# Depthwise-separable 1x1: preparing the weights in PSUM or in SBUF, one pw load ahead of x, smaller first chunks

## The chip, the cores and the metric

The kernel runs on one core of a Trainium2 chip. The metric is the device time of one execution in microseconds (us); less is better. TensorE (PE) multiplies, VectorE (DVE), ScalarE (ACT) and GpSimd (POOL) work on elements, SyncE (SP) issues most of the transfers. A time or a view of the trace counts from the start of the profiled span.

## What is computed

With a depthwise kernel of 1x1 the reference is a scaling of the channels followed by a matrix product over them:

```python
# x: (1, 384, 384, 384) bf16, dw: (1, 1, 384) bf16, pw: (384, 384) bf16
out = x * dw[0, 0][None, None, None, :]
return jnp.einsum('bhwc,cd->bhwd', out, pw)
```

The kernel scales the weights instead of x: out = x @ (diag(dw) pw), 147,456 rows of 384 channels. x is 113 MB, and so is the output.

## The kernel before

The rows are done in steps of 512, called supertiles here, 288 of them. Of each, DVE transposes 32x32 blocks of channel pairs (a bf16 pair moves as one 32-bit word), so that channels come to lie on partitions; PE multiplies, four row groups of 32 partitions side by side; ACT copies the result from PSUM; SP loads x and stores the output in chunks of several supertiles.

The four row groups each need all weights on their own 32 partitions, and even and odd channels apart. So the kernel makes `w_r`, 128 partitions of 6 blocks x 2 parities x 384 columns, in which each quadrant of 32 partitions holds the same weights, already times dw. It makes all six blocks with PE: a selection matrix, scaled by dw, times the rows of pw, into PSUM, and from there to SBUF by ACT and DVE.

The chunks of the first supertiles, and the loads that come first:

```python
head, tail = [[1, 1, 2, 2, 4]], [[6, 4], [4, 1, 1, 1, 1]]   # supertiles per load; groups of 10 between
...
nc.scalar.dma_start(dw_row[:], dw...).then_inc(s_dw, 16)
nc.sync.dma_start(pw_n[:, 0], pw[0:P, :]).then_inc(s_pw, 16)
nc.sync.dma_start(pw_n[:, 1:3], pw[P:C, :].rearrange("(k p) d -> p k d", p=P)).then_inc(s_pw2, 16)
load_x(0)
...                                          # then the other x loads and the stores, in order
```

The order of the weights in a supertile on PE; 12 steps of four matmuls each:

```python
w_first = {(0, 0): [(0, 1), (1, 3)], (4, 0): [(1, 4)], (4, 1): [(1, 5)]}   # weights that must be there
steps = [(b, par) for b in range(4) for par in range(2)] + [(4, 0), (5, 0), (4, 1), (5, 1)]

def supertile(s, rv):
    for b, par in steps:
        for q in range(4):
            if q == 0 and par == 0 and b in (0, 3):
                nc.tensor.wait_ge(s_t[s][b // 3], rv)          # half of the transposed x
            if q == 0 and s == 0:
                for e, v in w_first.get((b, par), []):
                    nc.tensor.wait_ge(s_wr[e], v)
            mm = nc.tensor.matmul(PS[s][:, q, :D],
                lhsT=Ts[s][32*q : 32*q+32, b, par::2], rhs=w_r[32*q : 32*q+32, b, par, :], ...)
```

What PE does ahead of the first supertile. `idle_work` multiplies constants by constants, so that PE is busy:

```python
idle_work(4)
nc.tensor.wait_ge(s_dw, 16)
for k in range(3):                       # dw from a row to a column: three 1x1 products into PSUM
    ...
mm.then_inc(s_df)
idle_work(2)
nc.tensor.wait_ge(s_pw, 16)
times = {(2, 0): 2, (2, 1): 2}           # these are done twice over, with the same result
for k in range(3):
    if k == 1:
        nc.tensor.wait_ge(s_pw2, 16)
    nc.tensor.wait_ge(s_sw, k + 1)
    for r in range(2):
        if k == 2:
            nc.tensor.wait_ge(*w_done[r])
        for v in [0, 1] * times.get((k, r), 1):
            mm = nc.tensor.matmul(PS[(k + 1) % 2][:, 2 * r + v, :D],
                lhsT=sel_w[64*v : 64*v+64, k, r, :, :]..., rhs=pw_n[64*v : 64*v+64, k, :], ...)
        mm.then_inc(s_w)
```

DVE builds the selection matrices, and ACT (five times) and DVE (once) take two banks of PSUM at a time to `w_r`; then DVE transposes the first two supertiles:

```python
w_eng = [1, 0, 1, 1, 1, 1]               # 1: ACT, 0: DVE
...
nc.vector.wait_ge(s_df, 1)
nc.vector.tensor_copy(dw_f[:], PS[1][:, 0, D : D + 3]).then_inc(s_dwf)
nc.vector.wait_ge(s_dwf, 2)
for k in range(3):
    nc.vector.tensor_scalar_mul(sel_w[:, k], sel[:]..., dw_f[:, k : k + 1]).then_inc(s_sw)
for i in range(6):
    w_out(i)                             # w_r[:, 2k : 2k+2, r, :] <- PSUM, 128x768
transposes(*order[0])
transposes(*order[1])
```

In the main loop DVE transposes supertile j + 2 as soon as PE is through with the buffer of supertile j.

Of the kernel before, what the change touches and what calls it, by code (L numbers as in the profile page):

```python
# [8 lines left out]
F32 = mybir.dt.float32  # L9
# [3 lines left out]
LMAX = 10  # L13
# [4 lines left out]
def _groups(n_super: int):  # L18

    head, tail = [[1, 1, 2, 2, 4]], [[6, 4], [4, 1, 1, 1, 1]]  # L20
    mid = n_super - sum(map(sum, head + tail))
    assert mid > 0 and mid % LMAX == 0
    return head + [[LMAX]] * (mid // LMAX) + tail
# [3 lines left out]
def kernel(  # L27
# [12 lines left out]
    nc = tc.nc  # L40
    P = nc.NUM_PARTITIONS
    B, H, W, C = x.shape
    assert dw.shape[0] == 1 and dw.shape[1] == 1, "only k=1 depthwise supported"
    D = pw.shape[1]
# [10 lines left out]
    chunks, first = [], 0  # L55
# [19 lines left out]
    sel_w = raw[:, 3 * D :].rearrange("p (k r q w) -> p k r q w", r=2, q=4, w=32)  # L75
    w_k = raw[:, 0 : 2 * D].rearrange("p (r d) -> p r d", d=D)
    eye = consts.tile([P, P], BF16, name="eye")
    sel = consts.tile([P, 2, 32], F32, name="sel")
    w_r = consts.tile([P, NB, 2, D], BF16, name="w_r")
    dw_row = consts.tile([1, C], BF16, name="dw_row")  # L80
    dw_f = consts.tile([P, 3], F32, name="dw_f")
    warm = consts.tile([P, 2], F32, name="warm")
# [6 lines left out]
    Ts = [bufp.tile([P, NB, 256], BF16, name=f"T{i}") for i in range(2)]  # L89
    Os = [bufp.tile([P, 4 * LMAX * D], BF16, name=f"O{i}") for i in range(NR)]  # L90
    PS = [psum.tile([P, 4, 512], F32, name=f"ps{s}") for s in range(2)]

# [8 lines left out]
    s_o = [nc.alloc_semaphore(f"s_o{i}") for i in range(NR)]  # L101
    s_dw = nc.alloc_semaphore("s_dw")
    s_pw = nc.alloc_semaphore("s_pw")
    s_pw2 = nc.alloc_semaphore("s_pw2")
    s_df = nc.alloc_semaphore("s_df")
# [3 lines left out]
    s_w = nc.alloc_semaphore("s_w")  # L109
    s_wr = [nc.alloc_semaphore(f"s_wr{e}") for e in range(2)]  # L110

    with tc.tile_critical(sync_engine=mybir.EngineType.Pool, no_gpsimd_drain=True):  # L112
# [60 lines left out]

        w_eng = [1, 0, 1, 1, 1, 1]
        w_all = [(s_wr[e], w_eng.count(e)) for e in range(2)]

        nc.scalar.dma_start(dw_row[:], dw.rearrange("a e c -> a (e c)")).then_inc(s_dw, 16)
        nc.sync.dma_start(pw_n[:, 0], pw[0:P, :]).then_inc(s_pw, 16)  # L178
        nc.sync.dma_start(pw_n[:, 1:3], pw[P:C, :].rearrange("(k p) d -> p k d", p=P)).then_inc(s_pw2, 16)  # L179
        load_x(0)  # L180

        todo = []
# [5 lines left out]
        for _, f, a in sorted(todo, key=lambda a: a[0]):  # L188
            if f is load_x and chunks[a[0]][4] == LMAX and chunks[a[0]][0] == 1:
                nc.sync.wait_ge(x_of(1)[1], 16)  # L190
            if f is store and a == (0, 0):

                for _ in range(28):
                    nc.sync.wait_ge(s_pw, 16)
            f(*a)
# [7 lines left out]

        w_done = [(s_wr[e], w_eng[: i + 1].count(e)) for i, e in enumerate(w_eng)]

        w_first = {(0, 0): [(0, 1), (1, 3)], (4, 0): [(1, 4)], (4, 1): [(1, 5)]}

        def w_ps(i):
            return PS[0 if i in (2, 3) else 1][:, 2 * (i % 2) : 2 * (i % 2) + 2, :D]


        steps = [(b, par) for b in range(4) for par in range(2)] + [(4, 0), (5, 0), (4, 1), (5, 1)]

        def supertile(s, rv):
            for b, par in steps:
                for q in range(4):
                    if q == 0 and par == 0 and b in (0, 3):
                        nc.tensor.wait_ge(s_t[s][b // 3], rv)
                    if q == 0 and s == 0:
                        for e, v in w_first.get((b, par), []):  # L220
                            nc.tensor.wait_ge(s_wr[e], v)
                    mm = nc.tensor.matmul(  # L222
                        PS[s][:, q, :D],
# [23 lines left out]

        idle_work(4)

        nc.tensor.wait_ge(s_dw, 16)  # L250
        for k in range(3):
            mm = nc.tensor.matmul(
                PS[1][:, 0, D + k : D + k + 1],
                lhsT=dw_row[:, P * k : P * k + P],
                rhs=ones[0:1, 0:1],
                start=True,
                stop=True,
            )
        mm.then_inc(s_df)
        idle_work(2)  # L260
        nc.tensor.wait_ge(s_pw, 16)
        times = {(2, 0): 2, (2, 1): 2}
        for k in range(3):
            if k == 1:
                nc.tensor.wait_ge(s_pw2, 16)
            nc.tensor.wait_ge(s_sw, k + 1)
            for r in range(2):
                if k == 2:
                    nc.tensor.wait_ge(*w_done[r])

                for v in [0, 1] * times.get((k, r), 1):
                    mm = nc.tensor.matmul(  # L272
                        PS[(k + 1) % 2][:, 2 * r + v, :D],
                        lhsT=sel_w[64 * v : 64 * v + 64, k, r, :, :].rearrange("p q w -> p (q w)"),
                        rhs=pw_n[64 * v : 64 * v + 64, k, :],
                        start=True,
                        stop=True,
                        tile_position=(64 * v, 0),
                    )
                mm.then_inc(s_w)  # L280
        with nc.tensor.Fori(0, NS // 2 - 1, 1) as it:
# [21 lines left out]
        for m in range(4):  # L303
# [11 lines left out]


        nc.gpsimd.affine_select(  # L317
            out=eye[:],
# [5 lines left out]
            channel_multiplier=1,  # L324
        ).then_inc(s_sel)
        for sem, v in w_all:
            nc.gpsimd.wait_ge(sem, v)
# [9 lines left out]
        for s in range(2):  # L337
            nc.scalar.copy(warm[:, s : s + 1], nc.const_aps.tensor(0.0, [P, 1], F32)).then_inc(s_a[s])  # L338

        def transposes(t, j):  # L340
# [17 lines left out]
            for h in range(2):  # L358
                if h == 0 and j == 0:
                    nc.vector.wait_ge(sem, n)  # L360
                ins = nc.vector.transpose(  # L361
                    out=Tw[:, 3 * h : 3 * h + 3],
                    in_=Xw[:, :, j, 96 * h : 96 * h + 96].rearrange("p k (b w) -> p b k w", w=32),
                )
                if jj >= 2:
                    ins._wait_ge(s_pe, 2 * (jj - 2) + h + 1)
                ins.then_inc(s_t[s][h])
# [5 lines left out]

        def w_out(i):
            e, k, r = w_eng[i], i // 2, i % 2
            out, in_ = w_r[:, 2 * k : 2 * k + 2, r, :], w_ps(i)
            o = nc.vector.tensor_copy(out, in_) if e == 0 else nc.scalar.copy(out, in_)  # L377
            o._wait_ge(s_w, i + 1)
            o.then_inc(s_wr[e])

# [5 lines left out]
            axis=mybir.AxisListType.X,  # L386
        ).then_inc(s_dwf)
        nc.vector.wait_ge(s_df, 1)
        nc.vector.tensor_copy(dw_f[:], PS[1][:, 0, D : D + 3]).then_inc(s_dwf)
        nc.vector.wait_ge(s_dwf, 2)  # L390
        for k in range(3):
            nc.vector.tensor_scalar_mul(
                sel_w[:, k], sel[:].unsqueeze(2).to_broadcast([P, 2, 4, 32]), dw_f[:, k : k + 1]
            ).then_inc(s_sw)
        for i in range(6):
            w_out(i)
        transposes(*order[0])
        transposes(*order[1])

# [62 lines left out]
```

## Time and profile before

| | |
|---|---|
| time, median of three runs | 573.68 us (573.62 to 574.42) |
| span of the profiled run | 571.9 us |
| PE busy | 567.0 us (99%) |
| DVE busy | 505.4 us (88%) |
| ACT busy | 418.4 us (73%) |
| DMA, mean over the span | 397 GB/s |
| first main matmul (kernel line 222) | 6.52 us |

The shares of the page are averages over the span, and nearly all of it is the main loop. The change concerns the first microseconds, so the views by time count here: the chain of work that ended last, and the timeline of each engine. L222 is the main matmul, L361 the transpose, L377 the copy of the weights from PSUM, L272 the matmul that makes them, L178 and L179 the loads of pw, L389 the copy of dw from PSUM, L392 the scaling of the selection matrices. A name with q (SPq) is the engine's sequencer, which issues the loads.

### The profile page before, as it was taken

To read this page: it belongs to the slowest core of one execution; us is meant where nothing else is said; L and a number is where in the kernel's file an instruction comes from. 1 tells how busy PE (TensorE), PEld (TensorE's weight loads), DVE (VectorE), ACT (ScalarE), POOL (GpSimd) and SP (SyncE) were. 2 spreads that over 40 slices of the span, in tenths; PEclk is the share of its full clock that TensorE was granted. 3 is DMA by queue.
4 is the path that set the end of the run, shared out by engine and by line. 5 is a ranking of instruction groups with operands and counts; after the bars stand their busy time and mean duration, and the time that the engine had idled before them with its cause. 6 is when DMAs were issued, how large, how long until landed. Compare 5 with 4: busy or idle time off the path is not lost.

```text
span 571.9 us, 29705 instructions
## 1 busy us (share of the span) xinstructions
PE 567.0 (99%) x13843; PEld 380.0 (66%) x13843; DVE 505.4 (88%) x586; ACT 418.4 (73%) x298; POOL 13.9 (2%) x41
## 2 busy tenths in 40 slices
PE   9999999999999999999999999999999999999997
PEld 4666666666666666666666666666666666666664
DVE  6889889889889889889889889889889889889885
ACT  6777777777777777777777777777777777777775
POOL 2042000000000000000000000000000000000000
PEclk9999999999999999999999999999999999999999
DMA  8999999999999999999999999999999999998677
GB/s 328 445 393 414 426 416 428 437 426 411 430 416 420 388 396 432 388 390 396 433 382 396 418 415 408 397 416 414 395 403 428 387 394 402 420 393 351 285 287 263
DMA packets 26740, 226.88 MB, mean 397 GB/s; under 512 B 1385, under 2 KB 7274, under 8 KB 22890
## 3 DMA queue, kind: packets, MB, share of 16 engines
q1 hardware_dynamic: 25796, 225.91, 97.4%
q10 hardware_dynamic: 934, 0.89, 0.4%
q14 instruction: 9, 0.07, 0.0%
q8 instruction: 1, 0.02, 0.0%
HBM read 113.54 MB, written 113.25 MB: 397 GB/s over the span
## 4 chain that ended last, share of the span: by engine, by line
PE 98%; DMA 1%; SPq 0%; DVE 0%; issue 0%; ACT 0%; POOLq 0%
PE ps L222 98%; DMA X<-in_x_dram 1%; PE ps L307 0%; PE ps L295 0%; DVE T L361 0%; ACT O L416 0%; SPq L179 0%; SPq L178 0%; SPq L457 0%; POOLq L112 0%; POOLq L446 0%
## 5 line engine op out<-in xcount | busy, mean ns | idle before, releaser
L222 PE MATMUL ps<-w_r,T 32*128 32x384 bf16 x13776 | 559.8, 321 | 0.2 <-DVE T L361 0.2
L361 DVE STREAM_TRANSPOSE T<-X 128x384 uint32<-128x384 uint32 x572 | 498.1, 874 | 58.2 <-DMA X<-in_x_dram 2.1
L421 ACT CAST O<-ps 128x1536 bf16<-128x1536 f32 x286 | 411.4, 1438 | 147.0 <-PE ps L222 147.0
L222 PEld LDWEIGHTS ps<-w_r,T 32*128 32x128 bf16 x13776 | 377.2, 93 | 183.1 <-issue 0.9
L336 POOL COPY Xk<-Xl 32x256 bf16<-32x256 bf16 x16 | 6.3, 394 | 0.0
L335 POOL COPY Xk<-Xl 32x128 bf16<-32x128 bf16 x16 | 4.6, 287 | 25.2 <-DMA Xl<-in_x_dram 24.3
L377 ACT CAST w_r<-ps 128x768 bf16<-128x768 f32 x5 | 3.6, 820 | 0.8 <-PE ps L272 0.8
L330 POOL COPY raw<-w_r 32x768 bf16<-32x768 bf16 x4 | 3.3, 819 | 6.4 <-ACT w_r L377 6.2
L239 PE MATMUL ps<-const-bfloat16-1.0 32*128 32x384 bf16 x24 | 2.2, 516 | 1.1 <-PEq L446 1.1
L272 PE MATMUL ps<-raw 64*128 64x384 bf16 x16 | 2.9, 513 | 0.1
L338 ACT ACT_TABLE_LOAD x1 | 1.3, 1283 | 1.5 <-PEq L446 1.5
L272 PEld LDWEIGHTS ps<-raw 64*128 64x128 bf16 x16 | 0.8, 113 | 2.2 <-DMA raw<-in_pw_dram 1.2
L412 DVE CAST O<-ps 128x384 bf16<-128x384 f32 x2 | 1.0, 552 | 1.4 <-PE ps L222 1.4
L361 DVE STREAM_TRANSPOSE T<-Xl 128x384 uint32<-128x384 uint32 x2 | 1.8, 876 | 0.2
L239 PEld LDWEIGHTS ps<-const-bfloat16-1.0 32*128 32x128 bf16 x24 | 0.7, 117 | 1.4 <-issue 1.4
L349 DVE STREAM_TRANSPOSE T<-Xk 128x384 uint32<-128x384 uint32 x2 | 1.2, 578 | 0.5 <-PE ps L222 0.4
L382 DVE TENSOR_REDUCE sel<-eye 128x64 f32<-128x128 bf16 x1 | 0.3, 290 | 1.5 <-POOL eye L317 1.5
L307 PE MATMUL ps<-raw,T 128*128 128x384 bf16 x8 | 1.5, 327 | 0.0
L416 ACT CAST O<-ps 128x384 bf16<-128x384 f32 x2 | 1.0, 478 | 0.7 <-PE ps L307 0.7
L377 DVE CAST w_r<-ps 128x768 bf16<-128x768 f32 x1 | 1.0, 958 | 0.5 <-PE ps L272 0.5
L416 DVE CAST O<-ps 128x384 bf16<-128x384 f32 x2 | 1.1, 558 | 0.1
L411 ACT CAST O<-ps 128x384 bf16<-128x384 f32 x2 | 0.9, 482 | 0.5 <-PE ps L222 0.5
(13 smaller groups left out, 4.5 us busy)
## 6 DMA issues: line engine op xcount, KB each, us to landing
X<-in_x_dram SPq DMA_DIRECT2D x26, 3840.0 KB, 21.9
out_dram<-O SPq DMA_DIRECT2D x26, 3840.0 KB, 27.9
X<-in_x_dram SPq DMA_DIRECT2D x3, 1536.0 KB, 18.5
out_dram<-O SPq DMA_DIRECT2D x4, 768.0 KB, 7.7
out_dram<-O SPq DMA_DIRECT2D x2, 1536.0 KB, 13.7
X<-in_x_dram SPq DMA_DIRECT2D x1, 2304.0 KB, 20.2
out_dram<-O SPq DMA_DIRECT2D x1, 2304.0 KB, 11.1
X<-in_x_dram SPq DMA_DIRECT2D x4, 384.0 KB, 4.4
```

The source lines that it names most:

```text
L222: mm = nc.tensor.matmul(PS[s][:, q, :D], lhsT=Ts[s][32 * q : 32 * q + 32, b, par::2], rhs=w_r[32 * q : 32 * q + 32, b, par, :], start=(b, ...
L239: nc.tensor.matmul(PS[0][:, 2 * (i % 2) + i // 2, :D], lhsT=ones[32 * i : 32 * i + 32, 0:P], rhs=ones[32 * i : 32 * i + 32, :], start=True ...
L272: mm = nc.tensor.matmul(PS[(k + 1) % 2][:, 2 * r + v, :D], lhsT=sel_w[64 * v : 64 * v + 64, k, r, :, :].rearrange("p q w -> p (q w)"), rhs ...
L307: mm = nc.tensor.matmul(PS[1][:, m, :D], lhsT=Tk[:, P * (m + 2) : P * (m + 3), par], rhs=w_k[:, par, :], start=False, stop=par == 1,)
L330: nc.gpsimd.tensor_copy(w_k[quads[n]], w_r[quads[n], n]).then_inc(s_wk)
L335: nc.gpsimd.tensor_copy(Xk[quads[n], g:8:4, :], x_b).then_inc(s_xk)
L336: nc.gpsimd.tensor_copy(Xk[quads[n], 8 + g : 24 : 4, :], Xl[quads[g], :, 64 * n : 64 * n + 64]).then_inc(s_xk)
L338: nc.scalar.copy(warm[:, s : s + 1], nc.const_aps.tensor(0.0, [P, 1], F32)).then_inc(s_a[s])
L361: ins = nc.vector.transpose(out=Tw[:, 3 * h : 3 * h + 3], in_=Xw[:, :, j, 96 * h : 96 * h + 96].rearrange("p k (b w) -> p b k w", w=32),)
L377: o = nc.vector.tensor_copy(out, in_) if e == 0 else nc.scalar.copy(out, in_)
L416: o = (nc.scalar.copy if n % 2 else nc.vector.tensor_copy)(Ov[:, n, j, :], PS[s][:, n, :D])
L421: a = nc.scalar.copy(Ov[:, :, j, :], PS[s][:, :, :D])
```

## The change

Six things are changed, all ahead of or in the first supertiles:

1. The last third of pw (channels 256 to 383) no longer goes through PE and PSUM. It is loaded four times, once to each quadrant of 32 partitions (two loads from SP, two from ACT, into a part of an output buffer that isn't in use yet), and scaled in SBUF by DVE (even channels) and POOL (odd channels). The scales for it come from four tiny matmuls and a copy by ACT.
2. The other weights leave PSUM one bank at a time (128x384), six by ACT and two by DVE, and PE's first supertile waits for each block where it needs it; its order of blocks is changed to suit.
3. The first 256 rows of pw are one load, and x0 is issued right after it.
4. The scaling of the selection matrices reads dw from PSUM; the copy of dw is gone.
5. The first half of the first transpose is done in three pieces with a signal each.
6. The chunks of x at the start are smaller: 1, 1, 1, 1, 2, 4 and then 5, 5, in place of 1, 1, 2, 2, 4 and 10.

It is meant to let PE begin, and go through, the first supertile earlier. The diff, cut to its core:

```diff
-    head, tail = [[1, 1, 2, 2, 4]], [[6, 4], [4, 1, 1, 1, 1]]
+    head, tail = [[1, 1, 1, 1, 2, 4], [5, 5]], [[6, 4], [4, 1, 1, 1, 1]]
 ...
+    w_d = Os[2][:, 0 : 4 * D].rearrange("p (b e) -> p b e", b=2)
 ...
-        nc.sync.dma_start(pw_n[:, 0], pw[0:P, :]).then_inc(s_pw, 16)
-        nc.sync.dma_start(pw_n[:, 1:3], pw[P:C, :].rearrange("(k p) d -> p k d", p=P)).then_inc(s_pw2, 16)
+        nc.sync.dma_start(pw_n[:, 0:2], pw[0 : 2 * P, :].rearrange("(k p) d -> p k d", p=P)).then_inc(s_pw, 16)
         load_x(0)
+        def load_w(eng, q):
+            rows = pw[2 * P : C, :].rearrange("(b i r) d -> i b (r d)", b=2, r=2)
+            eng.dma_start(w_d[32 * q : 32 * q + 32], rows).then_inc(s_wd, 16)
+        for q in range(2, 4):
+            load_w(nc.sync, q)
 ...
+        w_first = {
+            (0, 0): [(0, 2), (1, 2)], (2, 0): [(1, 3)], (3, 0): [(1, 4)], (2, 1): [(1, 5)], (3, 1): [(1, 6)],
+            (4, 0): [(0, 3)], (4, 1): [(2, 1)], (5, 0): [(0, 4)], (5, 1): [(2, 2)],
+        }
+        steps = [(b, par) for b in range(2) for par in range(2)]
+        steps += [(2, 0), (3, 0), (2, 1), (3, 1)] + [(b, par) for b in (4, 5) for par in range(2)]
 ...                                                     # in supertile(), for the first one
+                        if par == 0 and b in (1, 2):
+                            nc.tensor.wait_ge(s_tb, b)
 ...                                                     # PE ahead of the first supertile
-        idle_work(4)
+        idle_work(3)
 ...
-        idle_work(2)
+        idle_work(4)
         nc.tensor.wait_ge(s_pw, 16)
-        times = {(2, 0): 2, (2, 1): 2}
+        times = {(1, 1): 4}
+        nc.tensor.wait_ge(s_sw, 1)
+        copies(0, 0)                                     # copies(k, r): the matmuls as before, into PS[k]
+        nc.tensor.wait_ge(s_sw, 3)
+        for r in range(2):
+            for v in range(2):                           # scales of the last third: four products of one column
+                mm = nc.tensor.matmul(PS[1][:, 2 + v, D + 4 + r : D + 5 + r], lhsT=sel_w[..., 2, r, ...], rhs=ones[...])
+        mm.then_inc(s_df)
+        copies(0, 1)
+        copies(1, 0)
+        nc.tensor.wait_ge(s_dk, 1)
+        copies(1, 1)
 ...                                                     # POOL
+        nc.gpsimd.wait_ge(s_dk, 1)
+        nc.gpsimd.wait_ge(s_wd, 64)
+        for b in range(2):
+            w_scale(nc.gpsimd, b, 1).then_inc(s_wr[2])
 ...                                                     # ACT, after its table load and two small copies
+        for q in range(2):
+            load_w(nc.scalar, q)
 ...                                                     # DVE, first supertile
+                if h == 0 and jj == 0:
+                    for b in range(3):
+                        x_b = Xw[:, :, 0, 32 * b : 32 * b + 32]
+                        nc.vector.transpose(out=Tw[:, b], in_=x_b).then_inc(s_tb if b else s_t[0][0])
+                    continue
 ...
-        nc.vector.tensor_copy(dw_f[:], PS[1][:, 0, D : D + 3]).then_inc(s_dwf)
         for k in range(3):
-                sel_w[:, k], sel[:]..., dw_f[:, k : k + 1]
+                sel_w[:, k], sel[:]..., PS[1][:, 3, D + k : D + k + 1]
-        for i in range(6):
-            w_out(i)
+        nc.scalar.wait_ge(s_df, 2)
+        nc.scalar.copy(dw_k..., PS[1][:, 2:4, D + 4 : D + 6]).then_inc(s_dk)
+        for b, r in ((0, 0), (0, 1), (2, 0), (3, 0), (2, 1), (3, 1)):
+            w_out(1, b, r)                               # ACT: w_r[:, b, r, :] <- one bank, 128x384
+        for r in range(2):
+            w_out(0, 1, r)                               # DVE
         transposes(*order[0])
+        nc.vector.wait_ge(s_dk, 1)
+        nc.vector.wait_ge(s_wd, 64)
+        for b in range(2):
+            w_scale(nc.vector, b, 0).then_inc(s_wr[0])   # w_r[:, 4+b, r, :] <- w_d[:, b, ...] * scale
         transposes(*order[1])
```

## The prediction, made before the changed kernel was run

> **What bounds the kernel now.** I read the page's shares first, then the chain of work that ended last in order of time, then the groups of the first 8.5 us, then the start engine by engine in the timeline, and last the waits of VectorE (DVE).
>
> The chain in order of time (columns: start us, length us, what):
>
> ```profile
> 0.96 0.39 SPq L178
> 1.41 0.41 SPq L179
> 1.87 3.94 DMA X<-in_x_dram
> 5.84 0.59 DVE T L361
> 6.52 559.85 PE ps L222 x12053
> ```
>
> After 6.52 us there is one unbroken piece of main matmuls. It can't be shortened by anything at the start; it can only begin earlier. What stands ahead of it is: two issues of pw, the load of x0 (3.94 us from issue to landing), and half of the first transpose. One 512-row step ("supertile") of the main loop is 12 weight steps of four matmuls side by side; 559.85 us over about 286.7 of them is 1.953 us each, so 0.163 us per weight step. The first supertile ran from 6.52 to about 8.47 us.
>
> The groups of the first 8.5 us, each shape by itself (after the bar: busy us, mean ns of one | idle us before):
>
> ```profile
> L377 ACT CAST w_r<-ps 128x768 bf16<-128x768 f32 x5 | 3.6, 820 | 0.8 <-PE ps L272 0.8
> L272 PE MATMUL ps<-raw 64*128 64x384 bf16 x16 | 2.9, 513 | 0.1
> L222 PE MATMUL ps<-w_r,T 32*128 32x384 bf16 x49 | 2.3, 324 | 0.2 <-DVE T L361 0.2
> L377 DVE CAST w_r<-ps 128x768 bf16<-128x768 f32 x1 | 1.0, 958 | 0.5 <-PE ps L272 0.5
> L392 DVE TENSOR_SCALAR raw<-sel,dw_f 128x256 bf16<-128x256 f32 x3 | 0.9, 350 | 0.0
> L389 DVE COPY dw_f<-ps 128x3 f32<-128x3 f32 x1 | 0.2, 163 | 0.9 <-PE ps L252 0.9
> ```
>
> Three things are to be seen. ScalarE (ACT) evicts five of six weight blocks, from 3.91 to 7.52 us, one every 0.69 us. TensorE (PE) takes 513 ns for a 384-column matmul while it makes the weights and 324 ns for one of the same width in the main loop: until about 6.6 us it runs at half rate. The matmul that starts at 5.8 us still takes 0.52 us, the four at 6.5 take 0.34 to 0.35, those from 6.7 take 0.32. (The clock column reads full there because it has no record for the first microseconds; the durations decide.) And in those 8.5 us the main matmuls waited once, for the transpose.
>
> The timeline of ACT and of DVE (start us, length us, engine, line, operation, count, idle before):
>
> ```profile
> 3.91 3.61 ACT L377 CAST w_r<-ps 128x768 bf16<-128x768 f32 x5 [0.80 <-PE ps L272]
> 24.71 536.73 DVE L361 STREAM_TRANSPOSE T<-X 128x384 uint32<-128x384 uint32 x552 [1.47 <-DMA X<-in_x_dram]
> ```
>
> The second line shows where loads come nearest to the stream: the first load of ten supertiles lands at 24.6 us, DVE waits 1.47 us for it, yet PE does not stop, since DVE is ahead of it. Supertile 10 begins at 6.52 + 10 x 1.953 = 26.05 us, and its first half is transposed by 24.71 + 0.88 = 25.6 us: 0.45 us of slack.
>
> **What the skill says.** "TensorE: Matmul & The Clock Gate", Part 1, has the array at half clock until it has been busy through a window of about 3.4 us that runs free of the kernel's start. The trace agrees in the two rates (513 and 324 ns, 0.32 against 0.163 us from one group of row-tiled matmuls to the next) and in a switch near 6.6 us; whether the moment is fixed it can't say. "DMA: Bandwidth & Descriptors", "Issuing engines are not separate DMA queues", says that loads from two engines share the same DMA engines, so the second queue saves issue time alone; the trace shows the shared side at 0.65 busy in the first 6.5 us and full from then on. "GPSIMD Engine Reference", section 3.1, gives a one-input loop 1.8 cycles an element at best, so 384 would be an estimated 0.58 us; the GpSimd (POOL) copies here agree or are a little faster: 0.29 us for 128 columns, 0.39 for 256, 0.82 for 768, so 0.50 us for 384 between them.
>
> **The change part by part.**
>
> *pw's 256 rows in one load, then x0.* One issue of about 0.45 us leaves SyncE's queue ahead of x0, which is then issued at 1.42 instead of 1.87 us, with 196 KB ahead of it instead of 295 KB. DMA moved some 230 GB/s between 2.2 and 4.5 us, so 98 KB fewer are 0.43 us; issue and bytes are the same gain, not two. x0 lands at about 5.81 - 0.45 = 5.4 us.
>
> *The first transpose in pieces.* The half that PE waits for took 0.58 us; its first third, an estimated 0.2 us, now releases PE. Together with the load, data would let PE begin at about 5.7 us instead of 6.52: up to 0.8 us.
>
> *What PE itself must do first.* Before the main loop PE does, at half rate, 0.32 us a group or pair: seven idle groups instead of six, of which four come after the dw matmuls; then pairs (0,0), four tiny matmuls for the scales, (0,1), (1,0), and (1,1) four times. The dw matmuls end near 2.4 us (the first ran at 2.38, behind the fourth idle group, which now comes later). Then 4 x 0.32 = 1.28 us of idle work to 3.7; (0,0) to 4.0; the tiny ones to 4.15; (0,1) and (1,0) to 4.8; (1,1) four times 0.32 to 6.1 us. The one wait among these, for the copy of the scales on ACT, should end near 4.6: ACT has then finished its two new load issues (about 0.5 us each behind 3.0 us). So PE reaches the first supertile at **about 6.1 us**, not 5.7: the padding sets the start now, not x0. Earliest start moves by 6.52 - 6.1 = 0.4 us.
>
> *Clock.* If full rate comes at 6.6 us as before, 0.5 us of the first supertile runs at half rate: 1.5 of its 12 weight steps are done by 6.6, the other 10.5 take 10.5 x 0.163 = 1.71 us, end 8.3 instead of 8.47. Of the 0.4 us, about 0.2 are left. If full rate comes earlier, the padding shrinks too and the gain is 0.4 to 0.5 us.
>
> *Evictions bank by bank.* A 128x384 copy by ACT takes 0.48 us elsewhere in this trace (groups of the last two supertiles) and 0.11 us of a copy overlaps the next one, as with the wide ones (0.80 long, 0.69 apart): one every 0.37 us. ACT: scales to 4.6, the first four copies to about 6.2, the last two after (1,1), which is complete at about 6.35: 6.8 and 7.2 us. PE needs the fifth at its seventh weight step (6.6 + 4.5 x 0.163 = 7.3) and the sixth one step later (7.5). Enough, by 0.3 us. DVE's two copies of 0.55 us lie between 4.2 and 5.3, ahead of x0.
>
> *The last third from SBUF.* Two loads of 98 KB stand behind x0 in SyncE's queue, two are issued from ACT at about 3.0 and 3.5 us. pw's first load took 2.0 us on an empty queue, x0's 3.9 behind others; I take 2.5 to 3.3 us, so all are there at 6.0 to 6.8. DVE is with the transposes until about 6.6, then does two scalings of 0.2 to 0.35 us (350 ns for 256 columns of f32 are the nearest row): 6.9 and 7.2; PE asks for the first at 7.6. POOL's two at 0.5 to 0.6 us each begin at 6.4 (6.0 to 6.8): the second ends at 7.5 (7.1 to 8.0), and PE asks for it at 8.1. So all is beside other work, but with 0.1 us of margin at the late end.
>
> *x1 and the smaller chunks.* By x1's end the DMA engines have moved 196 + 2 x 393 + 4 x 98 = 1375 KB instead of 1081; at 430 GB/s that is 0.7 us later at most: it landed at 6.78, now 7.2 to 7.5. DVE transposes half of it in 0.5 us: 7.7 to 8.0, and PE wants it at 8.3. The chunk of ten that is now two of five lands its first half near 24.6 + 0.7 - 1966/430 = 20.7 us, so the slack of 0.45 us, which an earlier start and 295 KB more would have used up, becomes several microseconds. This gives nothing back; it keeps the gain.
>
> **Sum.** Start 0.4 us earlier, about 0.2 of it lost to half rate (0 to 0.2), stalls in the first supertile an expected 0.05, tail unchanged because the last 28 supertiles are chunked as before: gain 0.25 to 0.3 us. 573.68 - 0.28 = **573.4 us**.
>
> **Rivals.** *One: everything arrives and the start moves by the data's 0.8 us* (572.9 us). For it: the load and the transposes were the whole chain ahead of 6.52. Against: the count of padding at 0.32 us each. It needs full rate by about 5 us. *Two: the last third comes late.* A load that lands at 7.5 us instead of 6.4 stops PE at the ninth weight step, delays the second transpose on DVE too, which waits behind the scalings in program order, and costs 0.5 to 0.8 us: 573.9 to 574.2 us. For it: four more loads in the stretch where DMA is filling, two of them behind ACT's table load of 1.28 us. Against: 0.8 us of margin on DVE. *Three: the clock is everything*: the moment of full rate wanders by more than the change moves, and the medians differ by 0.3 us either way: 573.4 to 574.0. For it: the three runs before lie 0.8 us apart. *Four: loads starve the stream in the first 40 us,* where DMA is full: 0.5 us or more. Against: the five-supertile chunks.
>
> **Range and chances.** Rival one gives the low side, two and three the high one; I give the main line and its clock variants 0.6, rival one 0.12, two and three 0.28 together. Range 572.8 to 574.1 us. Nothing in the change touches the 560 us of main matmuls, and 2% is 11.5 us, so within 2% has 0.98, with 0.01 on each side.
>
> **What would show it.** Right: the chain no longer has DMA X directly ahead of the main matmuls but PE's own weight matmuls; the first main matmul starts at 6.0 to 6.2 us with a duration above 0.4 us; the second supertile starts near 8.3. DVE's wait of 1.47 us at 24.7 is gone. Wrong: main matmuls of the first supertile with gaps released by POOL or DVE w_r, or by the load of pw (rival two); a start below 5.8 us (one); gaps in PE between 10 and 40 us (four). A change of over 1 us in either direction would mean that the unbroken piece itself changed, which I exclude.

## The result, and the profile after

The changed kernel is slower: 576.9 us in the median of six runs (575.5 to 577.78), where the kernel before had 574.16 in its six (573.62 to 575.16). The ratio is 1.0044, with a 95% interval of 1.0026 to 1.0061. The prediction was 573.4 us with a range of 572.8 to 574.1; the result lies above it. In the profiled run the span is 575.3 us, and the whole difference lies in two places: the first supertile, and the last store.

Lines of the changed kernel: L230 is the main matmul, L274 the matmul that makes weights, L412 their copy from PSUM, L340 the scaling of the last third, L395 and L397 the transposes, L465 the output copy; L180, L135 and L185 are the loads of pw's 256 rows, of x and of the last third.

The chain that ended last in the changed kernel, in order of time (start us, length us, what):

```profile
0.94 0.45 SPq L180
1.46 0.45 SPq L135
...
2.43 4.88 DMA O<-in_pw_dram
...
7.49 2.58 POOL w_r L340 x2
10.06 0.05 issue
10.11 558.04 PE ps L230 x13732
```

Before, x0's load and a transpose stood ahead of the main matmuls. Now the fourth load of the last third of pw stands there (issued at 2.43, landed at 7.31 us), and behind it POOL's two scalings. The unbroken piece begins at 10.11 us.

The groups between 4 and 11 us, each shape by itself (after the bar: busy us, mean ns of one | idle us before, and what ended it):

```profile
L230 PE MATMUL ps<-w_r,T 32*128 32x384 bf16 x68 | 3.3, 323 | 1.7 <-POOL w_r L340 1.1 <-issue 0.6
L340 POOL TENSOR_SCALAR w_r<-O,dw_k 128x384 bf16<-128x384 bf16 x2 | 2.6, 1292 | 6.1 <-DMA O<-in_pw_dram 6.1
L412 ACT CAST w_r<-ps 128x384 bf16<-128x384 f32 x6 | 2.5, 497 | 0.2 <-PE ps L274 0.2
L395 DVE STREAM_TRANSPOSE T<-X 128x128 uint32<-128x128 uint32 x3 | 0.7, 283 | 1.1 <-DMA X<-in_x_dram 1.1
L340 DVE TENSOR_SCALAR w_r<-O,dw_k 128x384 bf16<-128x384 bf16 x2 | 0.8, 418 | 0.0
```

One scaling takes POOL 1292 ns and DVE 418, and POOL had waited 6.1 us for the loads. PE's timeline in the same stretch shows how its first supertile fell apart:

```profile
6.85 1.65 PE L230 MATMUL ps<-w_r,T 32*128 32x384 bf16 x36 [0.63 <-issue]
8.89 0.51 PE L230 MATMUL ps<-w_r,T 32*128 32x384 bf16 x8 [0.39 <-POOL w_r L340]
10.11 2.13 PE L230 MATMUL ps<-w_r,T 32*128 32x384 bf16 x48 [0.71 <-POOL w_r L340]
```

PE's weight matmuls had ended at 6.2 us. It began the first supertile only at 6.85, because x0 landed at 6.42 and the first piece of the transpose ended at 6.72; the view names no releaser there ("issue"). Then come nine weight steps of four matmuls, a wait for POOL's first block, two steps, a wait for its second, and only then the last step, which runs on into the second supertile. ACT's first output copy marks the end of the first supertile. Before and after:

```profile
8.72 1.44 ACT L421 CAST O<-ps 128x1536 bf16<-128x1536 f32 x1 [1.20 <-PE ps L222]
10.50 1.44 ACT L465 CAST O<-ps 128x1536 bf16<-128x1536 f32 x1 [3.38 <-PE ps L230]
```

That is 1.78 us. From there on the supertiles take 1.95 us each in both kernels.

The other place is the end. The chain's view doesn't show it; the transfers in the window from 571 to 575 us do (the window in 40 slices of 0.1 us; then queues with packets, MB and share of 16 engines; then the last store, issued at 570.75 us):

```profile
GB/s 307 399 323 338 384 300 323 330 448 323 300 146 8 0 0 0 0 0 8 8 15 8 8 8 23 23 23 0 0 0 0 0 0 0 0 0 0 0 0 0
...
q8 instruction: 1, 0.02, 1.5%
...
out_dram<-O ACTq DMA_DIRECT2D x1, 96.0 KB, 3.4
```

A fetch of instructions (16 KB, on queue 8, from 571.89 to 572.86 us) falls among the last packets. From 572.26 us no data moves for 0.6 us, and from 572.84 on, when the fetch ends, sixteen packets of 768 bytes come one by one, the last eight of them from the last store. It lands 3.4 us after its issue. In the kernel before, where the last store is issued at 568.97 us, the window from 568.5 to 572 us has no such fetch:

```profile
q10 hardware_dynamic: 144, 0.10, 9.0%
...
out_dram<-O ACTq DMA_DIRECT2D x1, 96.0 KB, 1.9
```

1.78 us at the start and 1.5 at the end make the 3.3 us by which the two spans differ (571.94 and 575.27).

### The profile page after: what moved, and what is told of

It reads as the page before. It is cut to its first block, busy times and chain, and to the rows that moved or that the text cites. A ratio compares the mean times of both kernels' runs of the same rounds, so it can differ in the third digit from the quotient of the medians.

```text
span 575.3 us, 30023 instructions
## 1 busy us (share of the span) xinstructions
PE 567.3 (99%) x13849; PEld 363.1 (63%) x13849; DVE 491.1 (85%) x590; ACT 417.6 (73%) x300; POOL 16.4 (3%) x43
## 4 chain that ended last, share of the span: by engine, by line
PE 97%; DMA 1%; POOL 0%; SPq 0%; issue 0%; ACT 0%; POOLq 0%
PE ps L230 97%; DMA O<-in_pw_dram 1%; POOL w_r L340 0%; PE ps L328 0%; PE ps L316 0%; ACT O L460 0%; SPq L180 0%; SPq L135 0%; SPq L185 0%; SPq L501 0%; POOLq L115 0%; POOLq L352 0%; POOLq L490 0%
## 5 line engine op out<-in xcount | busy, mean ns | idle before, releaser
L230 PE MATMUL ps<-w_r,T 32*128 32x384 bf16 x13776 | 560.2, 321 | 1.7 <-POOL w_r L340 1.1
L397 DVE STREAM_TRANSPOSE T<-X 128x384 uint32<-128x384 uint32 x571 | 482.7, 875 | 72.9 <-PE ps L230 72.9
L465 ACT CAST O<-ps 128x1536 bf16<-128x1536 f32 x286 | 411.7, 1439 | 148.9 <-PE ps L230 148.9
L230 PEld LDWEIGHTS ps<-w_r,T 32*128 32x128 bf16 x13776 | 360.1, 93 | 202.1 <-POOL w_r L340 1.9
L340 POOL TENSOR_SCALAR w_r<-O,dw_k 128x384 bf16<-128x384 bf16 x2 | 2.6, 1292 | 6.1 <-DMA O<-in_pw_dram 6.1
L412 ACT CAST w_r<-ps 128x384 bf16<-128x384 f32 x6 | 2.5, 497 | 0.2 <-PE ps L274 0.2
L274 PE MATMUL ps<-raw 64*128 64x384 bf16 x14 | 2.5, 514 | 0.0
L397 DVE STREAM_TRANSPOSE T<-Xl 128x384 uint32<-128x384 uint32 x2 | 1.7, 878 | 0.3 <-PE ps L230 0.3
L412 DVE CAST w_r<-ps 128x384 bf16<-128x384 f32 x2 | 1.0, 553 | 0.8 <-PE ps L274 0.8
L395 DVE STREAM_TRANSPOSE T<-X 128x128 uint32<-128x128 uint32 x3 | 0.7, 283 | 1.1 <-DMA X<-in_x_dram 1.1
L274 PEld LDWEIGHTS ps<-raw 64*128 64x128 bf16 x14 | 0.8, 121 | 1.3 <-DMA raw<-in_pw_dram 0.6
```

The source lines that it names most:

```text
L230: mm = nc.tensor.matmul(PS[s][:, q, :D], lhsT=Ts[s][32 * q : 32 * q + 32, b, par::2], rhs=w_r[32 * q : 32 * q + 32, b, par, :], start=(b, ...
L274: mm = nc.tensor.matmul(PS[k][:, 2 * r + v, :D], lhsT=sel_w[64 * v : 64 * v + 64, k, r, :, :].rearrange("p q w -> p (q w)"), rhs=pw_n[64 * ...
L340: return eng.tensor_scalar_mul(w_r[:, 4 + b, r, :], w_d[:, b, D * r : D * r + D], dw_k[:, k : k + 1])
L397: ins = nc.vector.transpose(out=Tw[:, 3 * h : 3 * h + 3], in_=Xw[:, :, j, 96 * h : 96 * h + 96].rearrange("p k (b w) -> p b k w", w=32),)
L412: o = copy(w_r[:, b, r, :], PS[b // 2][:, 2 * r + b % 2, :D])
L465: a = nc.scalar.copy(Ov[:, :, j, :], PS[s][:, :, :D])
```

## The experiments

All edits are small, so that one thing at a time is undone or done alone. Below, "first copy" is the start of ACT's first output copy, the end of the first supertile.

**Where POOL's time goes.** The main theory: POOL is far slower at a scaling than taken, and holds the first supertile.

*Run 3, the odd channels of the last third scaled by ACT:*

```diff
-        for b in range(2):
-            w_scale(nc.gpsimd, b, 1).then_inc(s_wr[2])
+        for b in range(2):        # ACT, after its six copies and the same waits
+            nc.scalar.mul(w_r[:, 4 + b, 1, :], w_d[:, b, D : 2 * D], dw_k[:, 2*b+1 : 2*b+2]).then_inc(s_wr[2])
```

> The changed kernel with the odd channels of the last third scaled by ScalarE instead of GpSimd (two instructions after its six copies). Theory: GpSimd's two scalings of 1.3 us each, 7.49 to 10.05 us, are what holds the first supertile; with ScalarE at about 0.5 us each, from 7.4, both are done by 8.4 and the first supertile ends near 8.7 to 8.9 instead of 10.4: 1.5 us less than the changed kernel, still with the late store in some executions. Rival (the late loads of the last third, landing at 7.3 us, are the cause by themselves): at most 0.5 us less.

Measured: 574.7 us in the median, lowest 573.63, ratio to the kernel before 1.0009 (0.9993 to 1.0025). ACT's and PE's timelines in its trace:

```profile
7.07 1.13 ACT L434 ACTIVATE w_r<-O,dw_k 128x384 bf16<-128x384 bf16 x2
8.64 1.44 ACT L465 CAST O<-ps 128x1536 bf16<-128x1536 f32 x1 [0.45 <-PE ps L230]
```

```profile
6.21 6.11 PE L230 MATMUL ps<-w_r,T 32*128 32x384 bf16 x137
```

Both scalings take ACT 1.13 us together. PE starts at 6.21 us and doesn't stop; the first copy is at 8.64. In the median 2.2 of the 2.7 us are back. Not all of that is POOL's: in this trace the last weight load landed at 6.74 us instead of 7.31, and there is no late fetch at the end. The engine's share shows beside runs 16 and 17 below, in which POOL scales: their last weight loads landed at 6.68 and 6.58 us, about as here, and their first copies start at 9.89 and 9.71. That is 1.1 to 1.25 us for POOL in ACT's place.

The first copy at 8.64 is 0.08 us earlier than in the kernel before, whose first copy lies at 8.66 and 8.85 us in the little changed forms of runs 5 and 2: in this trace, where nothing is late, the change with ACT in POOL's place gains next to nothing.

*Run 4, DVE idle beside POOL:*

```diff
         transposes(*order[0])
+        nc.vector.wait_ge(s_wr[2], 2)
         nc.vector.wait_ge(s_dk, 1)
```

> The changed kernel with one wait more: VectorE does its own scalings and the second transpose only after GpSimd has done both of its own, so nothing runs on VectorE beside them. It asks what the 1.3 us of one GpSimd scaling are. Theory (GpSimd's own speed at a scaling by a column of scales, 128x384): still 1.2 to 1.35 us each. Rival (it is held off the memory port that it shares with VectorE): 0.5 to 0.7 us each, as its copies of 0.29 us for 128 columns and 0.82 us for 768 suggest. The time of the whole kernel is expected 0.5 to 1 us over the changed one's, and says nothing here.

The groups of its trace between 5 and 11 us:

```profile
L340 POOL TENSOR_SCALAR w_r<-O,dw_k 128x384 bf16<-128x384 bf16 x2 | 2.5, 1246 | 5.0 <-DMA O<-in_pw_dram 5.0
L340 DVE TENSOR_SCALAR w_r<-O,dw_k 128x384 bf16<-128x384 bf16 x2 | 0.6, 318 | 2.4 <-POOL w_r L340 2.4
```

1246 ns, with DVE idle but for the first 0.14 us, against 1292 beside it. The rival came from the Trainium skill, "SBUF — State Buffer", "SBUF: two separate sides": for some VectorE operations, VectorE and GpSimd share a pair of ports, and the one that starts first holds the other off for its whole instruction. DVE's scaling does lengthen beside POOL, from 0.32 to as much as 0.56 us in the changed kernel's trace. But POOL loses at most the 0.1 us by which the first of its two was longer beside DVE (1.35 against 1.25 us). The rest is POOL's own: 3.2 ns a column, where its copies of 128 and 768 columns (0.29 and 0.82 us) differ by 0.83 ns a column. Those copies are on 32 partitions, the scalings on 128; no run separates the operation from the partitions. (The kernel itself took 575.65 us in one run.)

**The loads.** *Run 8, ACT's two weight loads moved to SP's queue:*

```diff
-        for q in range(2, 4):
+        for q in range(4):
             load_w(nc.sync, q)
...
-        for q in range(2):
-            load_w(nc.scalar, q)
```

> The changed kernel with ScalarE's two weight loads moved to SyncE's queue behind x0, so that none is ahead of x0 or beside it. Theory (ScalarE's loads, issued at 1.6 us under its table load instead of after it, took x0's bandwidth): x0 lands at 5.3 to 5.5 us instead of 5.95 and 6.42; the last weight load lands at 7.0 to 7.5, so GpSimd still ends near 10 and the time is that of the changed kernel, 575.2 to 577 us. Rival (x0's landing wanders by itself): x0 anywhere from 5.4 to 6.4.

Measured: 576.77 us (575.93 to 577.76), ratio 1.0035 (1.0013 to 1.0057). In its trace x0 lands at 5.74 us, not at the 5.3 to 5.5 expected. The rival fits: in the eleven traces that open with the changed kernel's loads (the changed kernel and runs 1, 3, 4, 6 and 13 to 18) x0 lands anywhere from 5.36 to 6.99 us, and 5.74 lies among them. That ACT's loads cost x0 time is not shown. As the theory had it, the last weight load lands at 7.38 us and POOL begins at 7.55; the last store is late here as well (3.7 us).

*Run 7, the order of the loads alone, in the kernel before:*

```diff
-        nc.sync.dma_start(pw_n[:, 0], pw[0:P, :])...
-        nc.sync.dma_start(pw_n[:, 1:3], pw[P:C, :]...)...
+        nc.sync.dma_start(pw_n[:, 0:2], pw[0 : 2 * P, :]...)...
         load_x(0)
+        nc.sync.dma_start(pw_n[:, 2], pw[2 * P : C, :])...     # PE waits for it at its third part
```

> The kernel before with the order of loads of the change alone: 256 rows of pw in one load, x0, then the last 128 rows of pw. Theory of the prediction: x0 lands 0.45 us earlier, near 5.4, the first main matmul starts near 6.1 to 6.2 instead of 6.52, part of it at half rate, 0.2 us gained: 573.7 to 574.0 us. Rival (x0's landing is set by the memory's slow first microseconds and not by what is ahead of it): x0 at 5.7 to 5.9 as before and no gain, 574.0 to 574.3 us.

Measured: 576.14 us (574.72 to 577.23), ratio 1.0038 (1.0024 to 1.0052). Both expectations missed: x0 does land earlier, at 5.14 us, and the kernel is 2 us slower. Its trace is of the shortest execution, and PE's timeline shows what that one lost:

```profile
4.12 2.95 PE L272 MATMUL ps<-raw 64*128 64x384 bf16 x16 [0.82 <-DMA raw<-in_pw_dram]
```

The one load of 256 rows landed at 4.07 us, where the first 128 rows had landed at 2.97 before; PE made the weights 0.75 us later, and the first copy is at 9.48, 0.76 later. *Run 11* is the same kernel again, for a longer execution's trace:

> The seventh run's kernel once more, for a second trace: its times lay from 574.7 to 577.2 us and the trace was of the lowest. Theory (loads land late by chance): where this execution is longer than 574.7 us, pw, x0, the last rows of pw or x1 land later by about as much, and the first output copy comes later than 9.5 us by about as much. Rival (the scatter is at the end): the first output copy is near 9.5 us and the last store takes over 2.5 us.

It took 576.1 us. PE's timeline from 3 to 12 us, and the group of main matmuls between 6 and 9.9 us:

```profile
3.61 1.46 PE L272 MATMUL ps<-raw 64*128 64x384 bf16 x8 [0.31 <-DMA raw<-in_pw_dram]
6.07 1.46 PE L272 MATMUL ps<-raw 64*128 64x384 bf16 x8 [1.00 <-DMA raw<-in_pw_dram]
7.46 4.80 PE L222 MATMUL ps<-w_r,T 32*128 32x384 bf16 x84
```

```profile
L222 PE MATMUL ps<-w_r,T 32*128 32x384 bf16 x32 | 2.7, 510 | 0.0
```

x0 landed at 4.71, but the last 128 rows of pw, now behind it, at 6.02 us. PE stood for a microsecond. And the main matmuls, which began at 7.46, took 510 ns instead of 324: full rate came only at 9.96 us, 3.4 us later than the 6.6 us of the kernel before. The first copy is at 10.85 us, 2.1 us later than before, though PE began the first supertile only 0.9 us later: the half rate cost the other 1.2 us. That PE's standing caused the late switch would fit the Trainium skill's page "TensorE: Matmul & The Clock Gate", Part 1, where full rate needs PE busy through a window of about 3.4 us; here it is one trace, and the link is not shown.

*Run 10, 256 and 128 rows of pw with x0 behind both, in the kernel before:*

```diff
-        nc.sync.dma_start(pw_n[:, 0], pw[0:P, :])...
-        nc.sync.dma_start(pw_n[:, 1:3], pw[P:C, :]...)...
+        nc.sync.dma_start(pw_n[:, 0:2], pw[0 : 2 * P, :]...)...
+        nc.sync.dma_start(pw_n[:, 2], pw[2 * P : C, :])...     # PE waits for it at its third part
         load_x(0)
```

> The kernel before with pw loaded as 256 and 128 rows instead of 128 and 256, x0 behind both as before. It takes one half of the seventh run. Theory (the one load of 256 rows makes PE's first product wait, and lands anywhere from 3.4 to 4.1 us): first eviction by ScalarE at 4.2 to 4.7 us instead of 3.9, median 574.3 to 576 with scatter as in the seventh run. Rival (it is x0 ahead of the last 128 rows that costs): 573.9 to 574.2 us as before.

Measured: 574.5 us (574.1 to 576.46), ratio 1.0014 (1.0008 to 1.0021). It costs 0.5 us, but not as expected: ACT's first eviction starts at 4.09 us, 0.2 later than before. In its trace x0 lands at 6.72 us, 0.9 later, with the same bytes ahead of it. So by the medians the one load of 256 rows goes with 0.5 of run 7's 2.1 us, and x0 ahead of the last rows with the rest; run 7's own trace shows a loss of the first kind, run 11's one of the second.

*Run 9, run 3's kernel with pw's 256 rows in two loads ahead of x0:*

```diff
-        nc.sync.dma_start(pw_n[:, 0:2], pw[0 : 2 * P, :]...).then_inc(s_pw, 16)
+        nc.sync.dma_start(pw_n[:, 0], pw[0:P, :]).then_inc(s_pw, 16)
+        nc.sync.dma_start(pw_n[:, 1], pw[P : 2 * P, :]).then_inc(s_pw2, 16)
         load_x(0)                                # PE waits for s_pw2 ahead of copies(1, 0)
```

> The changed kernel with the odd channels scaled by ScalarE, as in the third run, and with the 256 rows of pw in two loads of 128, both ahead of x0. Theory (with ScalarE the first supertile is no longer held; what is left over the kernel before, 0.6 us in the median, is the scatter of landings, and the one load of 256 rows is what scatters): median 573.6 to 574.2, little over 575. Rival (the extra loads of the last third scatter by themselves): 574.3 to 575 us in the median and single executions over 577, as in the third run.

Measured: 575.2 us (574.43 to 577.34), ratio 1.0028 (1.002 to 1.0037). The theory fell: the one load of 256 rows is not what is left. Whether two loads are worse than one, the intervals of this run and run 3 don't tell, since they overlap. In its trace x0, issued 0.4 us later and now behind the first of ACT's loads, lands at 7.25 us, the last weight load at 7.90, and the first copy is at 9.87. *Run 18* is run 3's kernel again:

> The third run's kernel (odd channels scaled by ScalarE) once more; its times lay from 573.6 to 578.3 us and the trace was of a short one. Theory (the rest of the loss is late loads at the start, amplified where PE's full clock comes later, or the late fetch at the end): in a longer execution than 574.3 us, the first output copy comes later than 8.7 us with the last weight load landing later than 6.8, or the last store takes over 3 us. Rival: neither.

575.2 us: x0 lands at 6.99, the last weight load at 8.11, the first copy is at 9.78, the last store takes 1.9 us. PE's timeline:

```profile
7.43 4.79 PE L230 MATMUL ps<-w_r,T 32*128 32x384 bf16 x108 [1.27 <-issue]
```

PE waited 1.27 us for x0 and its transpose, and from then on didn't stop. The theory held, and no clock was needed for it: full rate had come at 5.9 us. Late landing, of x0 here, costs this kernel a microsecond in such an execution.

**The chunks and the transpose.** *Run 5, the smaller chunks alone in the kernel before; run 6, the old chunks in the changed kernel:*

```diff
-    head, tail = [[1, 1, 2, 2, 4]], ...          # run 5; run 6 the other way round
+    head, tail = [[1, 1, 1, 1, 2, 4], [5, 5]], ...   # and in run 5 the change's condition for holding back a load
```

> The kernel before with the smaller chunks of x alone (1, 1, 1, 1, 2, 4 and 5, 5). Theory (all of the loss and of the scatter comes from the last third of the weights): 573.7 to 574.2 us, scatter as before, first output copy at 8.7 us, and VectorE's wait of 1.5 us at 24.7 us gone. Rival (the chunks bring the scatter, the changed kernel's executions lying 3 us apart): median over 575 us with highest values over 577.

> The changed kernel with the chunks of before (1, 1, 2, 2, 4 and 10). Theory (last third): as the changed kernel, 576.4 to 577.2 us in the median and as scattered, its first output copy 3.2 us after the last of the four weight loads has landed. Rival (chunks): back to 574 to 575 us with little scatter.

Run 5: 573.95 us, ratio 1.0002 (0.9994 to 1.001), first copy 8.66. Run 6: 577.08 us, ratio 1.0053 (1.0039 to 1.0067), first copy 11.03 us, 3.2 after the last weight load at 7.83. Both theories held. The chunks cost nothing and bring nothing by themselves; they take DVE's wait at 24.7 us away, which nothing waited for.

*Run 12, the first transpose in three pieces, in the kernel before:*

```diff
+                if h == 0 and jj == 0:
+                    for b in range(3): ...       # three transposes with a signal each, and PE's waits, as in the change
```

> The kernel before with the first half of the first transpose in three pieces, nothing else. Theory of the prediction: PE is released by the first piece 0.2 us after x0 has landed, if ScalarE's third copy (6.1 us) allows: first main matmul at 6.2 to 6.3 instead of 6.52, a part of it at half rate: 0.1 to 0.25 us less, 573.8 to 573.9 where the kernel before has 574.0. Rival: nothing measurable.

Measured: 573.85 us (573.44 to 574.15), ratio 0.9995 (0.9986 to 1.0003). No measurable gain. PE's timeline says why:

```profile
6.44 2.78 PE L225 MATMUL ps<-w_r,T 32*128 32x384 bf16 x64 [0.51 <-ACT w_r L385]
```

The wait for the transpose has become one for ACT's third copy of weights; the start moves from 6.52 to 6.44 us. (In this trace ACT's copies began at 4.09 us, 0.18 later than in the kernel before.)

**The late store.** Ahead of its first store SP passes 28 waits for a load of pw that has long landed; they only lengthen its stream of instructions. *Run 1, 16 of these padding waits instead of 28, in the changed kernel; run 2, 44 in the kernel before:*

```diff
-                for _ in range(28):
+                for _ in range(16):              # run 2: 44, in the kernel before
                     nc.sync.wait_ge(s_pw, 16)
```

> The changed kernel with 16 instead of 28 padding waits in SyncE's stream, nothing else. Theory (two causes): 1.8 us come from the first supertile, and about as much, in some executions only, from a 16 KB instruction fetch at 571.9 us that holds up one DMA engine and with it the last store. Fewer instructions on SyncE keep its stream short of the last fetch: no fetch of the kind late in the trace, the last store lands in under 2.2 us instead of 3.4, times 575.4 to 575.9 us with little scatter, about 1.0 to 1.5 us less in the median than the changed kernel; first output copy by ScalarE still at about 10.5 us. Rival (the late store is chance or the memory's): median and scatter stay, 575.5 to 577.8 us.

> The kernel before with 44 instead of 28 padding waits in SyncE's stream, nothing else. Theory: its stream then crosses the same boundary near the end, the trace shows a second 16 KB fetch near 570 us, and in half or more of the executions the last store is late: median 574.5 to 576 us, highest about 576. The start is as before (first main matmul near 6.5 us). Rival (the fetch has nothing to do with it): 573.6 to 574.4 us as before.

Run 1: 576.88 us (575.21 to 578.13), no better; run 2: 573.9 us (573.52 to 576.82), no worse, without a late fetch. The theory that the number of SP's instructions decides fell in this form. But run 1's trace (an execution of 575.66 us) had no late fetch, so its longer executions had to be seen. *Runs 13 to 15* are the changed kernel again, *16 and 17* that of run 1:

> The changed kernel itself once more, for a second trace. The kernel's times lie from 575.2 to 578.1 us; its trace so far shows 1.8 us at the start and, with one late last store, 1.5 us at the end. Theory one (late landing of the four weight loads, which decide when GpSimd begins): the first output copy comes 3.2 us after the last of them, and a longer execution has it later, 10.5 to 12 us. Theory two (full clock one window later, as in the eleventh run): the first main matmuls go on at 0.31 us a step until near 9.9 us, and the first output copy is 10.5 us or later although the loads landed by 7.3. Theory three (the end): the first output copy is near 10.5 us and the last store takes over 2.5 us, beside an instruction fetch of 16 KB.

> As the thirteenth run, a third trace: which of the three theories the longer of these executions show.

> As the thirteenth run, a fourth trace: which of the three theories the longer of these executions show.

> The first run's kernel (16 padding waits) once more, for a second trace; its times lay from 575.2 to 578.1 us, the trace was of a short one and had no late fetch. Theory (the late fetch comes in this kernel too, in some executions): where the execution is over 576.3 us, the trace shows a 16 KB fetch near 571.8 us and a last store of 3.4 to 3.7 us. Rival (something else lengthens these): no fetch, last store near 1.9 us, and the first output copy at 11 us or later.

> As the sixteenth run, a third trace of the same kernel: over 576.3 us either with a late fetch and a late last store, or with a late first output copy.

| trace | last weight load lands | first copy | last store takes | span |
|---|---|---|---|---|
| changed kernel | 7.31 | 10.50 | 3.4 | 575.3 |
| run 13 | 7.30 | 10.50 | 3.7 | 575.6 |
| run 14 | 7.53 | 10.72 | 3.5 | 575.6 |
| run 15 | 6.39 | 9.52 | 3.6 | 574.4 |
| run 1 | 7.15 | 10.35 | 1.9 | 573.6 |
| run 16 | 6.68 | 9.89 | 1.9 | 573.1 |
| run 17 | 6.58 | 9.71 | 3.6 | 574.7 |
| kernel before | none | 8.72 | 1.9 | 571.9 |

Two numbers rule the table. Where there are weight loads, the first copy comes 3.13 to 3.21 us after the last of them. And the span is the first copy plus 563.2 us where the last store takes 1.9 us, plus 564.8 to 565.1 where it takes 3.4 to 3.7; nothing else is needed to account for these spans. So in runs 13 to 15 theories one and three hold. Theory two doesn't: full rate came at 6.16, 6.83 and 5.69 us. Runs 16 and 17 are one kernel, without and with the late fetch; run 16 was too short an execution to test its theory, and in run 17 the late fetch and the late store came together. Their transfers at the end (from 570 to 575 us, run 16 first):

```profile
q14 instruction: 1, 0.01, 0.7%
...
out_dram<-O ACTq DMA_DIRECT2D x1, 96.0 KB, 1.9
```

```profile
q8 instruction: 1, 0.02, 1.5%
...
out_dram<-O ACTq DMA_DIRECT2D x1, 96.0 KB, 3.6
```

So one program has it in some executions and not in others. The late 16 KB fetch was in all four traces of the changed kernel, in run 8's, in one of the three of the kernel with fewer padding waits, and in none of the other fourteen traces; the last store took over 2.1 us in these six alone. In each of the six the fetch starts 1.10 to 1.14 us after the issue of the last store, takes 0.97 to 1.31 us, and the sixteen held packets resume within 0.02 us of its end. That it holds the store up is thus well supported; what decides whether it comes is not settled.

## Why the prediction was wrong

Of the 3.3 us in the traces, 1.78 lie at the start. There the prediction's sum failed at one term above all, in its paragraph on the last third: "POOL's two at 0.5 to 0.6 us each begin at 6.4", the second ending at 7.5 when PE asks for it at 8.1. They took 1.35 and 1.24 us, began at 7.49 and ended at 10.05. Two terms of that line were mis-sized:

- *The duration.* It was interpolated from POOL's copies, which are on 32 partitions, and an estimate of 0.58 us from the Trainium skill's best case for a loop ("GPSIMD Engine Reference", section 3.1: 1.8 cycles an element) seemed to agree. A scaling of 128 partitions by a column of scales is another operation: 3.2 ns a column, 1.25 us even with DVE idle. The error is 2.6 - 1.1 = 1.5 us. The chain of the changed kernel has both scalings in it, and run 3 shows PE without a gap once they are gone.
- *The landing.* 6.0 to 6.8 us was allowed; the last load came at 7.31 (6.39 to 7.53 in the further traces). It was the second of SP's two; ACT's two, issued at 1.61 and 2.00 us, under the table load and not behind it at 3.0, had landed by 6.17. The last load, issued at 2.43, took 4.9 us where 2.5 to 3.3 had been taken.

Run 15 parts the two: its last weight load landed at 6.39 us, as predicted, and its first copy, at 9.52, is still 0.8 us later than before. With these two, the start is explained. What happened is rival two, "the last third comes late", and with the sign that the prediction named: gaps in the first supertile that POOL's w_r ends. But it was taken as a matter of landing alone; its chance was too small, and its cost was put at 0.5 to 0.8 us, where it was 0.8 to 2.0 us in four traces.

The other 1.5 us, the late store, had no term in the sum at all. The prediction excluded a change of over 1 us, since only the unbroken piece could bring one. The measured loss is 2.7 us, and that piece is unchanged, at 1.95 us a supertile.

The other steps, against the trace of the changed kernel:

- *x0 at 5.4 us:* wrong there (6.42). The order alone does bring x0 forward, to 5.14 and 4.71 us in runs 7 and 11. That the one load of 256 rows ahead of it, or the rows of pw behind it, may come later was not in the sum, and cost more.
- *PE at the first supertile by 6.1 us:* right for PE's own work, whose last weight matmuls ended at 6.2. But then it waited for x0, and began at 6.85.
- *Pieces of the transpose:* 283 ns instead of 0.2 us each; without effect.
- *Evictions bank by bank:* right. The fifth and sixth started at 6.26 and 6.64 us and held nothing up.
- *Half rate until 6.6 us:* right in size (6.56 us in this trace by the clock record, 5.7 to 6.8 in the four of the changed kernel). That it can come as late as 9.96 us, as in run 11, was not foreseen. Rival three, that the clock is everything, fails all the same: full rate came at 8.17 us in run 16 and at 4.30 in run 17, and in both the first copy follows the last weight load as in the others.
- *Small chunks keep loads ahead:* right, and against rival four; PE has no gap after 11 us. x1 landed at 8.05 us instead of 7.2 to 7.5, without effect behind POOL.
- *"Tail unchanged":* wrong in the four traces of the changed kernel. The chunks of the tail are as before, but a fetch of instructions met the last store: 1.5 to 1.9 us. That the change itself brings this fetch is not shown.

The gain had been overrated as well: with nothing late (run 3's trace) the first supertile ends 0.08 us earlier, not 0.25 to 0.3. None of the versions tried beats the kernel before by more than the measurement can tell; runs 2 and 12 have the lowest ratios, 0.9994 and 0.9995, with 1 inside both intervals.

## What to carry to other kernels

Where a block of work is moved to another engine, its duration has to come from the same operation on that engine, not from a copy of like size; and where no row of the profile has it, the range must be as wide as that ignorance. A signal that waits for the last of several loads gets the latest of them: the last of the four added here landed anywhere from 6.2 to 8.1 us. A load moved forward can push back the ones behind it, as in run 11: look at which engine waits for those.

## What had not been expected of the hardware

In the first microseconds the transfers are slow: by 5.5 us 0.8 to 1.1 MB had been moved in the twenty traces, and by 7 us 1.1 to 1.6 MB; from 15 to 30 us it is 428 to 443 GB/s. Single packets of 3072 bytes, 0.12 us in the median later on, took up to 1.7 us there (run 4). x0's landing lay within 5.60 and 5.81 us in the four traces with the old order of loads (the kernel before, runs 2, 5 and 12), and between 4.7 and 7.3 us in all other orders. Whether the old order is steadier or four traces are too few is open.
